# Agent attention with an ELU layer on one Trainium2 core: both accumulators summed by VectorE, and 25 more split steps

## Chip, core and metric

The kernel runs on one core of one Trainium2 chip. The metric is the device time of one execution in microseconds (us). In what follows PE is TensorE's matmul stream, PEld its weight loads, DVE is VectorE, ACT ScalarE, POOL GpSimd, SP the queue that issues the transfers. L12 is line 12 of the kernel before, where nothing else is said.

## What is computed

Two batches of 12480 tokens of 128 channels, 49 agents per batch, and a layer of 128 to 2048 to 128 with an ELU between. All in fp32.

```python
def sm(a, b):
    s = scale * (a @ b.transpose(0, 2, 1))
    s = s - s.max(-1, keepdims=True)
    e = np.exp(s)
    return e / (e.sum(-1, keepdims=True) + 1e-09)
agent_v = sm(agents, k) @ v
x = (sm(q, agents) @ agent_v).reshape(B * S, D)
h = x @ w_in
g = np.where(h > 0.0, h, np.exp(np.minimum(h, 0.0)) - 1.0)
return g @ w_out
```

## The kernel before

**The algebra.** The 49 rows of agent_v are multiplied with w_in once per batch (A, 49 x 2048), so that the hidden layer of a token is A transposed times its 49 softmax weights p. What is left per token is the scores of q against the agents, their softmax, p times A, the ELU, and the product with w_out.

**Rounds, halves, steps.** A round j is 960 tokens, 13 rounds per batch, 26 in all. The 2048 hidden columns are taken in 16 blocks of 128. A round has two halves of 8 steps; step s of the 416 takes one pair of blocks, c = 0 to 7, for 480 tokens of two groups. In the loop at L720, slot s issues p1(s), the hidden-layer matmuls (L404 to L413: three products of the hi and lo parts, each as two matmuls on 49 rows that run side by side, so six records in three pairs), then p2(s - 4), the output matmuls of the step four slots back (L437 to L453), then the work on the other engines for step s. In elu ScalarE makes Relu of -h (L419) and Exp of minus that (L422), and VectorE joins them into g (L424, 960 elements on 128 partitions).

**Plain and split steps.** A plain step multiplies g by w_out in fp32 (w_f), four matmuls that show as 8 records. A split step cuts g into hi and lo parts in the fp32r format: VectorE casts hi (L431), GpSimd subtracts twice for lo (L204, 480 each), and p2 is twelve matmuls (hi with w_lo, hi with w_hi, lo with w_hi). Which steps are split is a table by c, SPLITS, and is_split (L401) picks its tuple.

**The end of a half.** p2 accumulates a half in two PSUM banks, o0 and o1, one for each 64-row group of TensorE. After c = 7 VectorE copies o1 to SBUF (ob, L465), ScalarE copies o0 (oa, L468, between Relu and Exp of the slot's step), GpSimd adds them (L469), and the result goes out by DMA. The first matmul of the next half, p2 of c = 0, overwrites both banks.

**What is done in between.** So that TensorE has work while the banks are read, the loop issues p1(s + 1) ahead of p2 of c = 0 in slots that are not in the set "covered". In the covered slots (L628 on) a visit stands there: scores of q or k, or the products with v, for a later round, at slots 16 i + 11 and others. The second halves of rounds with a visit end beside one, the others do not; 17 of the 51 boundaries are covered. Smaller work of the softmax hangs on slots by a table: mid (before elu in its slot) and pre (after it).

**Order.** The program is scheduled by hand: each engine runs its instructions in the order in which the code issues them, and waits for tiles that other engines write or still read. Hidden-layer results lie in three PSUM slots of two banks, o0 and o1 take the other two banks.

**The prologue** computes agent_v of batch 0 and A. Its odd score tiles and two of A's four quarters use o0 and o1 as scratch; A_part (L265, L275) writes the ahi and alo parts of a quarter.

Of the kernel before, what the change touches and what calls it, by code (L numbers as in the profile page):

```python
# [24 lines left out]
def tile_agent_attention_moe(  # L25
# [27 lines left out]
    SPLITS = ((1, 3, 4, 6, 7), (1, 4, 6, 7))  # L53
    SPLIT = tuple(c for c in range(NP) if c in SPLITS[0] or c in SPLITS[1])
    PLAIN = tuple(c for c in range(NP) if c not in SPLITS[0] or c not in SPLITS[1])
# [8 lines left out]
    wc_p = ctx.enter_context(tc.tile_pool(name="wc", bufs=2))  # L64
# [7 lines left out]
    pp = const.tile([TQ, R // 2, 128], F32)  # L72
    win_sb = big.tile([C, DFF], F32)
# [239 lines left out]
    def q_rz(j, half):  # L313
        z = q_st[j]["z"]
        if half == 0:
            nc.vector.scalar_tensor_tensor(out=z, in0=z, scalar=1e-9, in1=z, op0=ALU.add, op1=ALU.max)
        else:
            q_st[j]["z"] = sm_p.tile([TQ, R], F32, tag="z", name="z")
            nc.vector.reciprocal(out=q_st[j]["z"], in_=z)
# [96 lines left out]
    def elu(s, between=None):  # L416
# [3 lines left out]
        if between:  # L420
            between()
# [5 lines left out]
    def split(s):  # L427
# [3 lines left out]
        nc.vector.tensor_copy(out=hi_t[s], in_=g_t[s])  # L431
# [5 lines left out]
    def p2(s):  # L437
        j, half, c = at_step(s)
        if c == 0:
            o_t[0] = ps_o.tile([128, 512], F32, tag="o0", name="o0")  # L440
            o_t[1] = ps_o.tile([128, 512], F32, tag="o1", name="o1")
# [8 lines left out]
        for i, (w, v) in enumerate(jobs):  # L450
            for u, r in enumerate(ROWS):
                x = slice(r, r + 64)
                nc.tensor.matmul(out=o_t[u][:, 0:T], lhsT=w[x], rhs=v[x, :], start=first and i == 0, stop=last and i == len(jobs) - 1)  # L453
        if last:
            oa = o_p.tile([128, T], F32, tag="oa", name="oa")
            ob = o_p.tile([128, T], F32, tag="ob", name="ob")
            pa, pb = o_t[0], o_t[1]
            n = j * G + half * T
            if s == S - 1:
                for x in (slice(0, T // 2), slice(T // 2, T)):  # L460
# [20 lines left out]
    with tc.manual_schedule():  # L481
# [238 lines left out]
        for s in range(S + LAG):  # L720
# [12 lines left out]
            if x >= 0 and s != LEAD:  # L733
                after = p2(x)
# [45 lines left out]
```

## Time and profile before

| | |
|---|---|
| median of 3 runs | 998.0 us (997.5 to 999.86) |
| profiled execution, its own time | 998.71 us |
| its span, first to last instruction | 995.9 us |
| granted clock of TensorE, mean | 0.996 |
| PE busy | 978.3 us (98%) |
| PEld busy | 734.3 us (74%) |
| ACT busy | 884.3 us (89%) |
| DVE busy | 849.7 us (85%) |
| POOL busy | 687.0 us (69%) |

Busy times overlap between engines. A share near 100% says that an engine has no room; the chain of waits says which engines' work follows on one another up to the end. A row of a view by time gives the start, the duration, the engine, the line, the operation with what it writes and reads, how many instructions were joined in the row, and in brackets the idle time before it with the engine whose signal ended it. Joined rows overlap their neighbours, since matmuls are pipelined: the distance of two starts is the measure, not the duration.

### The profile page before, as it was taken

What the parts mean: (1) busy time and instruction counts of PE and PEld (TensorE: products, weight loads), DVE (VectorE), ACT (ScalarE), POOL (GpSimd) and SP (SyncE); (2) the same over time, 40 slices, a digit from 0 to 9 for tenths busy, and PEclk for the clock granted to TensorE, in tenths of its full rate; (3) what the DMA queues carried; (4) which work ended last, traced back from release to release, by engine and by line L of the source; (5) the groups of instructions that cost most, each with busy time, mean ns of one, the idle gap of its engine ahead of it and who ended that gap; (6) DMA issues with size and microseconds to landing.
All of it is one profiled execution on the core that took longest, in us unless ns stands there. A gap on an engine that the chain in (4) does not pass through costs nothing.

```text
span 995.9 us, 25483 instructions
## 1 busy us (share of the span) xinstructions
PE 978.3 (98%) x10380; PEld 734.3 (74%) x10380; DVE 849.7 (85%) x1028; ACT 884.3 (89%) x1017; POOL 687.0 (69%) x559
## 2 busy tenths in 40 slices
PE   7899999999999999999999999999999999999998
PEld 5767777777777777877777777777777777777775
DVE  7778888888888878888888898898888888988887
ACT  4588998988988889998998999989999989989996
POOL 3146666666666766766786886877868867867886
PEclk8999999999999999999999999999999999999999
DMA  9942222223232211101101101011020021001000
GB/s 349 385 148 89 80 72 81 78 74 96 68 85 66 66 41 46 38 31 65 36 23 55 37 26 62 26 56 41 18 76 27 21 66 37 26 12 37 27 20 21
DMA packets 25983, 67.30 MB, mean 68 GB/s; under 512 B 3083, under 2 KB 14963, under 8 KB 25867
## 3 DMA queue, kind: packets, MB, share of 16 engines
q1 hardware_dynamic: 25867, 65.69, 19.5%
q8 instruction: 81, 1.33, 0.6%
q14 instruction: 35, 0.29, 0.1%
HBM read 43.11 MB, written 12.78 MB: 56 GB/s over the span
## 4 chain that ended last, share of the span: by engine, by line
PE 93%; DVE 2%; ACT 2%; DMA 2%; issue 1%; POOL 0%; SPq 0%; DVEq 0%; ACTq 0%
PE o L453 59%; PE h L413 27%; PE h L291 2%; PE h L219 2%; PE h L160 1%; DMA v<-in_vx_dram 1%; PE h L331 1%; DVE g L424 1%; DMA k<-in_kT_dram 1%; ACT e L419 1%; ACT e L422 0%; PE o L160 0%; DVE m_all L168 0%; DVE ex L107 0%; ACT ex L103 0%
## 5 line engine op out<-in xcount | busy, mean ns | idle before, releaser
L204 POOL TENSOR_TENSOR lo<-g,hi 128x480 fp32r<-128x480 f32 x484 | 603.3, 1272 | 253.6 <-DVE hi L431 190.3
L424 DVE SCALAR_TENSOR_TENSOR g<-e,h 128x960 f32<-128x960 f32 x416 | 478.2, 1150 | 109.2 <-ACT e L422 91.7
L419 ACT ACTIVATE e<-h 128x960 f32<-128x960 f32 x416 | 402.5, 967 | 41.0 <-PE h L413 38.5
L422 ACT ACTIVATE e<-e 128x960 f32<-128x960 f32 x416 | 419.1, 1007 | 11.6
L453 PE MATMUL o<-g,w_f 64*128 64x480 f32 x1384 | 307.8, 562 | 0.2 <-DVE g L424 0.2
L413 PE MATMUL h<-py,ahi 49*128 49x480 f32 x832 | 292.4, 431 | 1.4 <-DVE g L424 0.7
L413 PE MATMUL h<-px,ahi 49*128 49x480 f32 x832 | 292.4, 431 | 0.1
L431 DVE CAST hi<-g 128x960 fp32r<-128x960 f32 x243 | 198.4, 816 | 10.8
L453 PEld LDWEIGHTS o<-g,w_f 64*128 64x128 f32 x1384 | 133.2, 185 | 83.1 <-issue 73.6
L413 PEld LDWEIGHTS h<-py,ahi 49*128 49x128 f32 x832 | 149.9, 186 | 39.3 <-issue 23.4
L413 PEld LDWEIGHTS h<-px,ahi 49*128 49x128 f32 x832 | 149.9, 186 | 26.3 <-issue 17.0
L453 PE MATMUL o<-hi,w_lo 64*128 64x480 f32 x972 | 159.4, 403 | 0.0
L413 PE MATMUL h<-px,alo 49*128 49x480 f32 x416 | 157.0, 377 | 0.0
L413 PE MATMUL h<-py,alo 49*128 49x480 f32 x416 | 157.0, 377 | 0.0
L453 PE MATMUL o<-lo,w_hi 64*128 64x480 f32 x972 | 146.9, 378 | 0.0
L453 PE MATMUL o<-hi,w_hi 64*128 64x480 f32 x972 | 146.0, 376 | 0.0
L453 PEld LDWEIGHTS o<-hi,w_lo 64*128 64x128 f32 x972 | 93.4, 186 | 26.0 <-issue 14.3
L453 PEld LDWEIGHTS o<-lo,w_hi 64*128 64x128 f32 x972 | 92.6, 184 | 13.6 <-POOL lo L204 0.3
L453 PEld LDWEIGHTS o<-hi,w_hi 64*128 64x128 f32 x972 | 92.5, 184 | 13.0
L413 PEld LDWEIGHTS h<-py,alo 49*128 49x128 f32 x416 | 76.6, 184 | 5.7
L413 PEld LDWEIGHTS h<-px,alo 49*128 49x128 f32 x416 | 76.6, 184 | 5.6 <-DVE alo L275 0.2
L469 POOL TENSOR_TENSOR ob<-ob,oa 128x480 f32<-128x480 f32 x51 | 70.0, 1372 | 12.2 <-ACT oa L468 12.2
(89 smaller groups left out, 517.7 us busy)
## 6 DMA issues: line engine op xcount, KB each, us to landing
k<-in_kT_dram SPq DMA_DIRECT2D x26, 480.0 KB
q<-in_qT_dram SPq DMA_DIRECT2D x26, 480.0 KB
out_dram<-ob SPq DMA_DIRECT2D x51, 240.0 KB
py<-px SPq DMA_DIRECT2D x104, 91.9 KB
v<-in_vx_dram SPq DMA_DIRECT2D x13, 516.0 KB
v<-in_vx_dram SPq DMA_DIRECT2D x13, 483.8 KB
raw<-in_w_in_dram SPq DMA_DIRECT2D x4, 512.0 KB
raw<-in_w_out_dram SPq DMA_DIRECT2D x4, 512.0 KB
```

The costliest lines, as they stand in the source:

```text
L160: nc.tensor.matmul(out=ps[u:u + w, j * NA:(j + 1) * NA], lhsT=src[:, x:x + w], rhs=ag_sb[:, b, :], start=True, stop=True)
L204: eng.tensor_tensor(out=out, in0=x, in1=hi.bitcast(F32), op=ALU.subtract)
L219: nc.tensor.matmul(out=ps[u:u + 64], lhsT=e[:, j * NA:j * NA + 64], rhs=v_t[b, r][:, j, :], start=(r == rs[0] and j < 2), stop=(r == rs[-1 ...
L291: nc.tensor.matmul(out=ps[u:u + w, t * NA:(t + 1) * NA], lhsT=src[:, x:x + w], rhs=ag_sb[:, j // NG, :], start=True, stop=True)
L331: nc.tensor.transpose(ps[:NA2, u, i * HP:(i + 1) * HP], pp[x, i, 0:NA2], ident[x, x])
L413: nc.tensor.matmul(out=h[:, u, 0:T], lhsT=a[x, :], rhs=p[u ^ half][x, :], start=i == 0, stop=i == 2)
L419: nc.scalar.activation(out=e, in_=h, func=ACTF.Relu, scale=-1.0)
L422: nc.scalar.activation(out=e, in_=e, func=ACTF.Exp, scale=-1.0)
L424: nc.vector.scalar_tensor_tensor(out=g, in0=e, scalar=-1.0, in1=h, op0=ALU.add, op1=ALU.max)
L431: nc.vector.tensor_copy(out=hi_t[s], in_=g_t[s])
L453: nc.tensor.matmul(out=o_t[u][:, 0:T], lhsT=w[x], rhs=v[x, :], start=first and i == 0, stop=last and i == len(jobs) - 1)
L469: nc.gpsimd.tensor_tensor(out=ob, in0=ob, in1=oa, op=ALU.add)
```

## The change

1. A third tuple in SPLITS, with c = 0 added, for the second half of rounds whose middle is not covered; covered rounds now take the longer of the old tuples in both halves. Split steps go from 243 to 268: 16 covered rounds gain c = 3 of the second half, 9 uncovered rounds gain c = 0 of the second half. Round 0 stays as it was.
2. The cast of these 25 steps (by_act) is issued for ScalarE, one slot later, after the Exp of the next step.
3. The accumulators are one tile of two banks. VectorE sums both in one reduce into ob (L468 of the new file), and the DMA follows. VectorE's copy, ScalarE's copy and GpSimd's add are gone; the very last boundary stays as it was.
4. elu of a slot comes ahead of its mid work.
5. The tiles of q's softmax stay in place and have a 50th column that is set to 1e-9 once; the sum runs over 50 columns, and the instruction that added 1e-9 (L316, once per round) goes.
6. The prologue's scratch is one tile "outer" in place of o0 and o1, so that readers and writers of its two banks wait for one another as of one tile. One more block of w_out is kept in hi and lo parts.

```diff
-    SPLITS = ((1, 3, 4, 6, 7), (1, 4, 6, 7))
+    SPLITS = ((1, 3, 4, 6, 7), (1, 4, 6, 7), (0, 1, 3, 4, 6, 7))
...
+    qe = [const.tile([TQ, R, NA + 1], F32, name=f"qe{i}") for i in range(2)]
...
-        nc.vector.tensor_reduce(out=q_st[j]["z"], in_=q_st[j]["e"], axis=AX.X, op=ALU.add)
+        nc.vector.tensor_reduce(out=q_st[j]["z"], in_=qe[j % 2], axis=AX.X, op=ALU.add)
...
-            nc.vector.scalar_tensor_tensor(out=z, in0=z, scalar=1e-9, in1=z, op0=ALU.add, op1=ALU.max)
...
     def is_split(s):
         j, half, c = at_step(s)
-        return c in SPLITS[half if j * NM + NP + LAG in covered else 0]
+        free = j * NM + NP + LAG not in covered
+        return c in SPLITS[2 if free and half else half if j == 0 else 0]
+
+    def by_act(s):
+        j, half, c = at_step(s)
+        return j > 0 and half == 1 and c == (EDGE if j * NM + NP + LAG in covered else 0)
...
-        nc.vector.tensor_copy(out=hi_t[s], in_=g_t[s])
+        if by_act(s):
+            cast_hi(nc.scalar, hi_t[s], g_t[s])
+        else:
+            nc.vector.tensor_copy(out=hi_t[s], in_=g_t[s])
...
-            o_t[0] = ps_o.tile([128, 512], F32, tag="o0", name="o0")
-            o_t[1] = ps_o.tile([128, 512], F32, tag="o1", name="o1")
+            o_t[0] = ps_o.tile([128, 2, 512], F32, tag="o", name="o")
...
-            nc.vector.tensor_copy(out=ob, in_=pb[:, 0:T])
-
-            def rest_of_sum():
-                nc.scalar.activation(out=oa, in_=pa[:, 0:T], func=ACTF.Copy)
-                nc.gpsimd.tensor_tensor(out=ob, in0=ob, in1=oa, op=ALU.add)
-                nc.sync.dma_start(out=outT[:, n:n + T], in_=ob)
-
-            return rest_of_sum
+            nc.vector.tensor_reduce(out=ob, in_=o[:, :, 0:T].rearrange("p u t -> p t u"), axis=AX.X, op=ALU.add)
+            nc.sync.dma_start(out=outT[:, n:n + T], in_=ob)
...
+            outer = ps_o.tile([128, 2, 512], F32, tag="o", name="o")
...
-            banks = [hk[:, 0, :], o_ps[0], o_ps[1], o_ps[0][:, 256:512]]
+            banks = [hk[:, 0, :], outer[:, 0, :], outer[:, 1, :], outer[:, 0, 256:512]]
...
+            if s < S:
+                elu(s)
             for fn, a in mid.pop(s, []):
                 fn(a)
-            if s < S:
-                elu(s, after)
-                split(s)
-            elif after:
-                after()
+            if 0 < s < S:
+                if by_act(s - 1):
+                    split(s - 1)
+                if not by_act(s):
+                    split(s)
```

ScalarE's order around the middle of round 23, one of the nine uncovered rounds, before: Relu and Exp of the second half's steps 0 to 3, the copy of o0 in the last. A name's number tells one tile from another.

```order
L419 ACTIVATE e_12467<-h_12448 128x960
L422 ACTIVATE e_12467<-e_12467 128x960
L419 ACTIVATE e_12483<-h_12472 128x960
L422 ACTIVATE e_12483<-e_12483 128x960
L419 ACTIVATE e_12513<-h_12494 128x960
L422 ACTIVATE e_12513<-e_12513 128x960
L419 ACTIVATE e_12540<-h_12518 128x960
L468 ACTIVATE oa_12537<-o0_12343 128x480
L422 ACTIVATE e_12540<-e_12540 128x960
```

The same place of the changed kernel:

```order
L421 ACTIVATE e_12538<-h_12519 128x960
L422 ACTIVATE e_12538<-e_12538 128x960
L421 ACTIVATE e_12554<-h_12543 128x960
L422 ACTIVATE e_12554<-e_12554 128x960
L199 ACTIVATE hi_12559<-g_12541 128x960
L421 ACTIVATE e_12590<-h_12571 128x960
L422 ACTIVATE e_12590<-e_12590 128x960
L421 ACTIVATE e_12617<-h_12595 128x960
L422 ACTIVATE e_12617<-e_12617 128x960
```

The cast of step 0 (hi from its g) now stands between Exp of step 1 and Relu of step 2; the copy of o0 is gone.

VectorE's order at the same boundary, before: g of steps 0 and 1, the cast of step 1, g of step 2, the copy of o1, g of step 3 and its cast.

```order
L424 SCALAR_TENSOR_TENSOR g_12470<-e_12467,h_12448 128x960
L424 SCALAR_TENSOR_TENSOR g_12486<-e_12483,h_12472 128x960
L431 CAST hi_12488<-g_12486 128x960
L424 SCALAR_TENSOR_TENSOR g_12516<-e_12513,h_12494 128x960
L465 COPY ob_12538<-o1_12344 128x480
L424 SCALAR_TENSOR_TENSOR g_12546<-e_12540,h_12518 128x960
L431 CAST hi_12548<-g_12546 128x960
```

And in the changed kernel:

```order
L424 SCALAR_TENSOR_TENSOR g_12541<-e_12538,h_12519 128x960
L424 SCALAR_TENSOR_TENSOR g_12557<-e_12554,h_12543 128x960
L434 CAST hi_12565<-g_12557 128x960
L424 SCALAR_TENSOR_TENSOR g_12593<-e_12590,h_12571 128x960
L468 TENSOR_REDUCE ob_12614<-o_12415 128x480
L424 SCALAR_TENSOR_TENSOR g_12620<-e_12617,h_12595 128x960
L434 CAST hi_12622<-g_12620 128x960
```

The reduce of both banks takes the place of the copy of one; it stays behind g of step 2.

TensorE's order there in the changed kernel: the end of the step pulled ahead, then the output matmuls of step 0, which were four plain ones (o0 and o1 from g_12470 and w_f) before.

```order
L415 MATMUL h_12635<-py0_11980,alo_6835 128x480
L415 MATMUL h_12635<-px0_11979,alo_6835 128x480
L456 MATMUL o_12642<-hi_12559,w_lo_89 128x480 x4
L456 MATMUL o_12642<-hi_12559,w_hi_88 128x480 x4
L456 MATMUL o_12642<-lo0_12561,w_hi_88 128x480 x2
L456 MATMUL o_12642<-lo1_12563,w_hi_88 128x480 x2
```

Step 0 is split here, and its first matmul waits for the reduce that reads the tile o.

## Rows read from the trace of the kernel before

**Rows 1.** The chain that ended last, its shares by line (page, part 4).

```profile
PE o L453 59%; PE h L413 27%; PE h L291 2%; PE h L219 2%; PE h L160 1%; DMA v<-in_vx_dram 1%; PE h L331 1%; DVE g L424 1%; DMA k<-in_kT_dram 1%; ACT e L419 1%; ACT e L422 0%; PE o L160 0%; DVE m_all L168 0%; DVE ex L107 0%; ACT ex L103 0%
```

**Rows 2.** Busy us from 700 to 900: PE, PEld, DVE, ACT, POOL; clock; DMA.

```profile
700.00:900.00 200.00, 200.00 (x1936) 149.65 (x1934) 176.41 (x201) 187.16 (x209) 152.23 (x121) 1.00 0.11 36
```

**Rows 3.** By time, PE from 887 to 893: three steps' first output matmuls.

```profile
887.99 1.77 PE L453 MATMUL o<-g,w_f 64*128 64x480 f32 x8
...
890.25 0.59 PE L453 MATMUL o<-hi,w_lo 64*128 64x480 f32 x4
...
892.20 0.59 PE L453 MATMUL o<-hi,w_lo 64*128 64x480 f32 x4
```

**Rows 4.** Groups by line and shape: count, busy us, mean ns, idle before.

```profile
L204 POOL TENSOR_TENSOR lo<-g,hi 128x480 fp32r<-128x480 f32 x484 | 603.3, 1272 | 253.6 <-DVE hi L431 190.3 <-PE h L413 32.2 <-DVE z L319 25.8
L424 DVE SCALAR_TENSOR_TENSOR g<-e,h 128x960 f32<-128x960 f32 x416 | 478.2, 1150 | 109.2 <-ACT e L422 91.7 <-POOL lo L204 6.0 <-PE h L413 3.8
...
L431 DVE CAST hi<-g 128x960 fp32r<-128x960 f32 x243 | 198.4, 816 | 10.8
...
L465 DVE COPY ob<-o 128x480 f32<-128x480 f32 x51 | 33.6, 658 | 2.6
...
L296 DVE TENSOR_REDUCE mx<-h 124x8 f32<-124x392 f32 x26 | 14.5, 558 | 0.0
...
L168 DVE TENSOR_REDUCE m_all<-h 120x49 f32<-120x392 f32 x20 | 10.9, 561 | 0.5
...
L172 DVE TENSOR_REDUCE mrun<-m_all 120x49 f32<-120x637 f32 x1 | 0.8, 814 | 0.0
```

**Rows 5.** By time, a boundary without a visit: PE's output matmuls, VectorE.

```profile
893.06 0.60 PE L453 MATMUL o<-lo,w_hi 64*128 64x480 f32 x4
...
894.81 1.77 PE L453 MATMUL o<-g,w_f 64*128 64x480 f32 x8
...
892.50 1.16 DVE L424 SCALAR_TENSOR_TENSOR g<-e,h 128x960 f32<-128x960 f32 x1 [0.32 <-ACT e L422]
893.73 0.66 DVE L465 COPY ob<-o 128x480 f32<-128x480 f32 x1
```

**Rows 6.** By time, PE after a wait: the first pair and the next.

```profile
70.18 0.48 PE L413 MATMUL h<-py,ahi 49*128 49x480 f32 x1
...
70.51 0.38 PE L413 MATMUL h<-py,ahi 49*128 49x480 f32 x1
```

**Rows 7.** By time, VectorE's copy at the first and the last such boundary.

```profile
101.34 0.66 DVE L465 COPY ob<-o 128x480 f32<-128x480 f32 x1
...
977.63 0.66 DVE L465 COPY ob<-o 128x480 f32<-128x480 f32 x1
```

**Rows 8.** By time, round 23's middle: ScalarE steps 1 to 3, VectorE 2.

```profile
906.21 1.01 ACT L422 ACTIVATE e<-e 128x960 f32<-128x960 f32 x1
907.47 0.97 ACT L419 ACTIVATE e<-h 128x960 f32<-128x960 f32 x1 [0.25 <-PE h L413]
908.48 1.01 ACT L422 ACTIVATE e<-e 128x960 f32<-128x960 f32 x1
909.43 0.98 ACT L419 ACTIVATE e<-h 128x960 f32<-128x960 f32 x1
...
909.58 1.15 DVE L424 SCALAR_TENSOR_TENSOR g<-e,h 128x960 f32<-128x960 f32 x1 [0.40 <-ACT e L422]
910.75 0.66 DVE L465 COPY ob<-o 128x480 f32<-128x480 f32 x1
```

**Rows 9.** By time, prologue's end: VectorE on A, PE's first output matmuls.

```profile
55.75 0.49 DVE L265 TENSOR_SCALAR ahi<-o,rz 113x256 fp32r<-113x256 f32 x1 [0.74 <-PE o L257]
56.27 0.48 DVE L275 SCALAR_TENSOR_TENSOR alo<-o,rz,ahi 113x256 fp32r<-113x256 f32 x1
56.67 0.48 DVE L265 TENSOR_SCALAR ahi<-o,rz 113x256 fp32r<-113x256 f32 x1
...
58.87 1.84 PE L453 MATMUL o<-g,w_f 64*128 64x480 f32 x7 [0.23 <-DVE g L424]
```

More of the change, by code (lines that the diff above doesn't have):

```diff
@@ L52, in tile_agent_attention_moe @@
     EDGE = (NP - 1 + LAG) % NP
-    SPLITS = ((1, 3, 4, 6, 7), (1, 4, 6, 7))
-    SPLIT = tuple(c for c in range(NP) if c in SPLITS[0] or c in SPLITS[1])
-    PLAIN = tuple(c for c in range(NP) if c not in SPLITS[0] or c not in SPLITS[1])
+    SPLITS = ((1, 3, 4, 6, 7), (1, 4, 6, 7), (0, 1, 3, 4, 6, 7))
+    SPLIT = (0, 1, 3, 4, 6, 7)
+    PLAIN = (0, 2, 3, 5)
     scale = 1.0 / float(C) ** 0.5
@@ L452, in p2 @@
                 x = slice(r, r + 64)
-                nc.tensor.matmul(out=o_t[u][:, 0:T], lhsT=w[x], rhs=v[x, :], start=first and i == 0, stop=last and i == len(jobs) - 1)
+                nc.tensor.matmul(out=o[:, u, 0:T], lhsT=w[x], rhs=v[x, :], start=first and i == 0, stop=last and i == len(jobs) - 1)
         if last:
-            oa = o_p.tile([128, T], F32, tag="oa", name="oa")
             ob = o_p.tile([128, T], F32, tag="ob", name="ob")
-            pa, pb = o_t[0], o_t[1]
             n = j * G + half * T
             if s == S - 1:
+                oa = o_p.tile([128, T], F32, tag="oa", name="oa")
+                pa, pb = o[:, 0], o[:, 1]
                 for x in (slice(0, T // 2), slice(T // 2, T)):
@@ L525, in tile_agent_attention_moe @@
             dve.memset(ones, 1.0)
+            for x in qe:
+                dve.memset(x, 1e-9)
             dve.memset(s_all[:, :, R:R + 1, :], 0.0)
@@ L607, in tile_agent_attention_moe @@
             av_out()
-            o_ps = [ps_o.tile([128, 512], F32, tag=f"o{i}", name=f"o{i}") for i in range(2)]
-            banks = [hk[:, 0, :], o_ps[0], o_ps[1], o_ps[0][:, 256:512]]
+            banks = [hk[:, 0, :], outer[:, 0, :], outer[:, 1, :], outer[:, 0, 256:512]]
             def A_part(c, eng):
@@ L729, in tile_agent_attention_moe @@
             if s == 2:
-                t = ps_o.tile([128, 512], F32, tag="o1", name="o1")
-                nc.tensor.matmul(out=t[:, 0:T], lhsT=ident, rhs=win_sb[:, 0:T], start=True, stop=True)
+                nc.tensor.matmul(out=outer[:, 1, 0:T], lhsT=ident, rhs=win_sb[:, 0:T], start=True, stop=True)
             x = s - LAG + (s < LEAD)
             if x >= 0 and s != LEAD:
-                after = p2(x)
+                p2(x)
             if s == NP - LAG - 1:
                 p1(s)
+            if s < S:
+                elu(s)
             for fn, a in mid.pop(s, []):
                 fn(a)
-            if s < S:
-                elu(s, after)
-                split(s)
-            elif after:
-                after()
+            if 0 < s < S:
[3 more added lines that the diff above has]
+                    split(s)
             for fn, a in pre.pop(s, []):
```

27 lines of the change are left out of this document (10 added, 17 removed).

## The prediction, written before the result was known

> **What bounds the kernel now.** I read the chain of waits first: it says which engine's work ends last. Two lines of TensorE hold 86% of it, the output matmuls (L453) with 59% and the hidden-layer matmuls (L413) with 27% [rows 1]. Then the busy time by stretch, since a chain can hide engines that are nearly full: from 700 to 900 us TensorE is busy for all of the 200 us, at a granted clock of 1.00, while ScalarE has 187, VectorE 176 and GpSimd 152 [rows 2]. So TensorE's own work sets the time, and nobody makes it wait in the steady state. What the change does is worth what it takes off TensorE's list of matmuls, less each wait that it opens on TensorE. The other three engines count only where one of them is late at one spot. Those spots I read in time order, engine by engine, at the end of an accumulation, which I call a boundary: the last output matmul of a half, the copy out of PSUM, and the first output matmul of the next half, which writes the same banks.
>
> **The change, part by part**, against the profiled execution (998.71 us; the median is 998.0, 0.7 lower).
>
> *25 more split steps.* Split steps rise from 243 to 268. A step of plain fp32 lasts 2.26 us on TensorE from the start of its output matmuls to the next step's (887.99 to 890.25), a split one 1.95 (890.25 to 892.20) [rows 3]. Each conversion takes 0.31 off, so 25 x 0.31 = **-7.8 us**.
>
> *The sum of the two banks on VectorE.* Before, VectorE copied one bank and ScalarE the other, side by side, and GpSimd added. Now one VectorE instruction reads both banks, 960 elements per partition in place of 480, and only then may TensorE write them again. Its duration is not in this trace. Below it lies the copy of 480, 0.66 us [rows 4], if only the outputs counted. Above it I put twice the nearest estimate, 2.3, if picking elements from two banks in turn halved the rate. The nearest rows: VectorE's reduces take 0.561 for 392 elements and 0.814 for 637, a slope of 1.03 ns per element, so 960 come to 0.814 + 323 x 1.03 ns = 1.15; and its two-operand pass over 960 takes 1.150 [rows 4]. I take 1.15. The reduce in L168 reads its 392 elements 49 apart, the one in L296 side by side, and they take 561 and 558 ns [rows 4], so a stride by itself is not seen to cost.
>
> What TensorE has as cover: at a boundary without a visit, the program pulls the hidden matmuls of one more step ahead. The last output matmul ends at 893.06 + 0.60 = 893.66, the copy starts at 893.73 (0.07 later), and the next output matmul at 894.81, 1.15 after that end [rows 5]. A matmul that has waited pays its weight load in the open: after a wait the first pair of matmuls is 0.33 from the next (70.18 to 70.51) [rows 6], against 0.22 in the flow (1.95 for the nine pairs of a split step [rows 3]), so 0.11; with 0.07 for the hand-over that is 0.18. The stall is 0.07 + 1.15 + 0.18 - 1.15 = 0.25 us. Boundaries without a visit lie between 101.34 and 977.63 [rows 7], 34 of the 51: 34 x 0.25 = **+8.5 us**. At the other 17 a visit's matmuls stand between as well; I cost those at nothing. If that cover were only as long as the pulled step, they would add 17 x 0.25 = 4.
>
> *The cast on ScalarE.* The added cast goes to ScalarE, behind the Exp of the step after. In 16 rounds it is step 3 beside a visited boundary, where ScalarE no longer has the copy and the visit leaves room: nothing. In 9 rounds it is step 0 of the second half, and there ScalarE's queue is: Exp of step 1, the cast, Relu and Exp of step 2; and VectorE's is: g of step 2, then the sum. Now Exp of step 1 starts at 906.21 and Relu of step 2 at 907.47. One full-width instruction follows another after 0.95 (908.48 to 909.43), so with a cast of that length Relu of step 2 starts at 906.21 + 0.95 + 0.95 = 908.11, 0.64 late [rows 8]. Exp and g of step 2 hang on it: g starts at 909.58 after waiting for that very Exp, and the copy follows at 910.75 as soon as g is done [rows 8]. So the sum starts 0.64 late, on top of its own stall, straight onto TensorE: 9 x 0.64 = **+5.8 us**. Lower bound 0 (if VectorE took the sum first, which its fixed order excludes), upper bound 9 x 1.0.
>
> Here the page "ScalarE: Activation LUTs" of the Trainium skill, section "Rules for kernel authors", speaks against the change: plain element-wise work belongs on VectorE, not ScalarE. This trace agrees with its direction, 0.66 to 0.82 for the cast on VectorE against 0.95 here. By that rule the cast would have stayed on VectorE and the time would be that of the second rival below.
>
> *The prologue.* The scratch of two banks is now one tile, so the matmuls for the fourth quarter of A wait for VectorE's alo of the third (56.27 + 0.48 = 56.75), and VectorE then waits for them, for some 0.74 as it did for the third [rows 9]. Its next step starts at 57.49, not 56.67, and TensorE already waits for the first g behind it (0.23 at 58.87): **+0.8 us**, lower bound 0.
>
> *At nothing.* GpSimd: 50 more lo at 1.27 = 64 us [rows 4], spread over the run, and 51 adds over as many elements are gone. VectorE: 51 x (1.15 - 0.66) = 25 us more, of the 24 idle in each 200. The guard of the softmax's sum by a 50th column, one small VectorE instruction fewer in each round, and the order of the mid-slot work behind g sit in that idle time. If VectorE's idle were gone, g would be late for the output matmuls four steps on, which none of these is long enough to reach.
>
> **Sum:** -7.8 + 8.5 + 5.8 + 0.8 = +7.3 on 998.71; against the median, 998.0 + 7.3 = **1005.3 us**.
>
> **The rivals.**
> - *The sum is quick, and the change is faster.* If VectorE's sum lasts about as long as the copy (0.66), the 34 boundaries cost nothing; the point from which it decides is 1.15 - 0.07 - 0.18 = 0.90 us. In the 9 rounds 0.07 + 0.64 + 0.66 + 0.18 - 1.15 = 0.40 is left: -7.8 + 3.6 + 0.8 = -3.4, so 994.6, and 991.0 if the cast's delay is hidden as well. For it: the copy is 0.66. Against it: both reduces and the two-operand pass follow the elements read.
> - *Only the cast's delay is hidden.* -7.8 + 8.5 + 0.8 = +1.5: 999.5, no change that can be told. For it: ScalarE loses its 51 copies, and each stall on TensorE lets it catch up. Against it: the fixed order [rows 8] has 0.25 idle before that Relu and no more.
> - *Two banks read in turn halve the rate.* 2.3 us: a stall of 1.40 at 34 boundaries, 47.6; -7.8 + 47.6 + 5.8 + 0.8 = +46.4, so 1044.4. Against it: the strided reduce above. The page "Advanced Engine Details and Errata" of the Trainium skill, section "PSUM Cachelines", says that every two neighbouring fp32 should lie side by side for best throughput; the sum's pairs lie 2 KB apart. L168's reduce breaks that rule too, at 561 ns against the 558 of one that keeps it, so no slowdown shows here.
> - *GpSimd is late for the added steps.* In the 9 rounds its pair for step 0 starts at about 908.1 and two pairs last 5.1, to 913.2; the matmuls that read the second come near 914.6. 1.4 us are spare; if a pile-up ate them and 0.5 more, 9 rounds would lose 4.5: 1009.8.
>
> **How the numbers follow.** A measurement of this kernel tells about 0.3%, 3 us, from no change. The forecast gets 0.52, the quick sum 0.15, the hidden cast 0.20, the two banks 0.05, GpSimd 0.08. Faster than 995: 0.12 of the quick sum and 0.04 of the hidden cast, together 0.16. Within 3 us: 0.03 + 0.14, and 0.05 of the forecast's low end (a sum of 1.05 us takes 3.4 off), 0.22. Slower: the rest, 0.62. The range leaves out the two banks and the lower part of the quick sum and goes from 994 to 1011, where the upper end is the forecast with a sum of 1.3 us (+5.1). The likeliest case's own range is 1001 to 1011.
>
> **What would show it.** In the changed profile: the sum's group near 1150 ns; TensorE idle of some 0.25 before the first output matmul of a half, put down to VectorE's sum, 34 times, and near 0.9 in the 9 rounds; split steps at 1.95; busy time of L456 plain matmuls down by 25 steps. Wrong would be a sum below 0.90, TensorE without idle at boundaries, or Relu of step 2 in its old place although the cast stands ahead of it.

## The result and the profile after

The changed kernel takes **1007.32 us** (median of 4 runs, 1007.07 to 1007.85), against 998.13 for the kernel before: a ratio of 1.009, with a 95% interval from 1.0073 to 1.0107. It is 9.2 us slower, in the direction forecast and inside the range; the sum of the terms had 7.3. The profiled execution took 1007.07 us with a span of 1005.3, 9.4 more than before.

The chain that ended last in the changed kernel, first by engine and then by line:

```profile
PE 76%; ACT 9%; DVE 8%; issue 5%; DMA 1%; POOL 1%; SPq 0%; DVEq 0%; ACTq 0%; POOLq 0%
PE o L456 48%; PE h L415 21%; ACT e L421 4%; ACT e L422 3%; PE h L219 2%; DVE g L424 2%; DVE ob L468 2%; PE h L291 2%; DVE hi L434 2%; PE h L160 1%; PE h L328 1%; ACT hi L199 1%; DMA k<-in_kT_dram 1%; DVE m_all L168 0%; ACT qe L307 0%
```

TensorE's two lines had 86% of it [rows 1]; now they have 69%, and ScalarE, VectorE and gaps ("issue") have the rest: TensorE is made to wait. Busy time hides that almost entirely. In the same stretch as [rows 2], with the same columns:

```profile
700.00:900.00 200.00, 199.26 (x1946) 157.84 (x1944) 179.72 (x191) 184.97 (x200) 149.02 (x121) 1.00 0.11 36
```

199.26 of 200 looks full, because a matmul's record is longer than its turn (0.38 us against 0.22) and its tail covers part of a wait. The waits have to be read from starts. I therefore compared both traces step by step, by the start of the first matmul on alo of each of the 416 steps (a record that is complete in both). What grows between two neighbouring steps is lost there. Grouped by the place, in us, with the experiments that follow:

| kernel | up to round 1 | c = 3 split, 16 places | first boundary, 18 rounds | first boundary, 7 uncovered rounds | second boundary, 9 uncovered rounds | rest | sum |
|---|---|---|---|---|---|---|---|
| changed | 1.2 | -4.5 | 4.3 | 5.0 | 3.1 | 0.0 | 9.1 |
| e1 old splits | 2.0 | 0.1 | 4.4 | 1.5 | 2.0 | -0.3 | 9.7 |
| e3 casts on VectorE | 3.9 | -4.7 | 4.2 | 1.6 | 5.2 | -0.3 | 9.9 |
| e4 no c = 3 | 4.5 | 0.3 | 4.4 | 1.5 | 3.2 | -0.2 | 13.7 |
| e5 half a sum | 0.8 | -4.4 | 0.1 | 1.9 | -0.2 | 0.0 | -1.8 |
| e8 prologue | 0.7 | -4.4 | 4.3 | 4.8 | 3.1 | -0.1 | 8.4 |
| e9 c = 3 early, old sum | 0.1 | -2.9 | -0.1 | 0.0 | 0.0 | -0.3 | -3.1 |
| e12 combined | 0.8 | -4.5 | 4.3 | 1.6 | 3.1 | -0.3 | 4.9 |

The first boundary is the one inside the first half of a round, the second the one in its middle; all of those counted have no visit. The second boundary's column includes the gain of c = 0's split, where there is one. The first column also holds when a trace's first loads landed, some tenths to 1.5 us either way: e6 and e11, whose prologue is that of the kernel before, have 1.6 and 1.5 there.

Groups of the changed kernel, as in [rows 4] (count, busy us, mean ns, idle before):

```profile
L204 POOL TENSOR_TENSOR lo<-g,hi 128x480 fp32r<-128x480 f32 x534 | 667.6, 1277 | 277.5 <-DVE hi L434 172.5 <-ACT hi L199 71.4 <-DVE z L316 21.8
...
L434 DVE CAST hi<-g 128x960 fp32r<-128x960 f32 x243 | 227.9, 938 | 13.2 <-DVE g L424 0.5
...
L468 DVE TENSOR_REDUCE ob<-o 128x480 f32<-128x960 f32 x51 | 58.9, 1155 | 0.7
...
L199 ACT ACTIVATE hi<-g 128x960 fp32r<-128x960 f32 x25 | 24.8, 991 | 0.0
```

The sum takes 1155 ns (the estimate was 1.15 us), the cast on ScalarE 991, and VectorE's 243 casts have grown from 816 to 938 on average although they are the same in number.

A boundary without a visit and without added steps near it, as in [rows 5]: TensorE's last and next output matmul, VectorE's g of step 2 and the sum.

```profile
934.56 0.62 PE L456 MATMUL o<-lo,w_hi 64*128 64x480 f32 x4
936.43 1.88 PE L456 MATMUL o<-g,w_f 64*128 64x480 f32 x8
...
934.04 1.16 DVE L424 SCALAR_TENSOR_TENSOR g<-e,h 128x960 f32<-128x960 f32 x1 [0.42 <-ACT e L422]
935.22 1.16 DVE L468 TENSOR_REDUCE ob<-o 128x480 f32<-128x960 f32 x1
```

The matmul ends at 935.18, the sum runs from 935.22 to 936.38, and the next output matmul starts at 936.43, 1.25 after that end in place of 1.15. The first group also lasts 1.34 up to the next (937.77) in place of 1.23 (896.04 against 894.81 in the trace before): the weight load in the open. Together 0.21.

**The first boundary of an uncovered round** (round 23) loses 0.64. The lines of GpSimd, VectorE, ScalarE, the last output matmul and the weight loads, in this order:

```profile
887.54 5.18 POOL L204 TENSOR_TENSOR lo<-g,hi 128x480 fp32r<-128x480 f32 x4 [4.45 <-ACT hi L199]
893.73 2.40 POOL L204 TENSOR_TENSOR lo<-g,hi 128x480 fp32r<-128x480 f32 x2 [1.01 <-DVE z L316]
...
894.92 1.72 DVE L434 CAST hi<-g 128x960 fp32r<-128x960 f32 x1
896.56 2.21 DVE L424 SCALAR_TENSOR_TENSOR g<-e,h 128x960 f32<-128x960 f32 x2
898.80 0.94 DVE L434 CAST hi<-g 128x960 fp32r<-128x960 f32 x1
899.90 1.16 DVE L424 SCALAR_TENSOR_TENSOR g<-e,h 128x960 f32<-128x960 f32 x1 [0.16 <-ACT e L422]
900.98 1.15 DVE L468 TENSOR_REDUCE ob<-o 128x480 f32<-128x960 f32 x1
...
896.36 1.01 ACT L422 ACTIVATE e<-e 128x960 f32<-128x960 f32 x1
897.80 0.97 ACT L421 ACTIVATE e<-h 128x960 f32<-128x960 f32 x1 [0.43 <-DVE g L424]
...
899.89 0.60 PE L456 MATMUL o<-lo,w_hi 64*128 64x480 f32 x4
...
901.11 0.18 PEld L415 LDWEIGHTS h<-px,ahi 49*128 49x128 f32 x1 [0.37 <-DVE g L424]
902.18 0.30 PEld L456 LDWEIGHTS o<-g,w_f 64*128 64x128 f32 x4 [0.55 <-DVE ob L468]
```

Read it from the top. GpSimd gets the pair for c = 3 only when ScalarE has cast it, and is late with the pairs after it. VectorE's cast of c = 7 at 894.92 then falls beside a running pair (893.73 to 896.13) and lasts 1.72 instead of 0.66. The two g behind it start at 896.56; ScalarE, which needs a buffer that this g frees, waits 0.43; so g of step 2 ends at 901.06, and the sum begins 0.49 after the last output matmul (900.49). TensorE waits twice: 0.24 for a hidden-layer slot that the late g frees (the load at 901.11), and then 0.40 at the sum.

That a cast stands still beside GpSimd's subtraction agrees with the Trainium skill, "SBUF — State Buffer", section "Who interferes with whom": VectorE and GpSimd share one pair of ports under an exclusive lock, and a cast can be among the VectorE instructions that want it. Here the cast ends about 0.5 after GpSimd's pair does, having stood for about 1.1.

**The second boundary** of the same round (c = 0 split, its cast on ScalarE), as in [rows 8]; ScalarE, VectorE, GpSimd, TensorE:

```profile
913.68 1.01 ACT L422 ACTIVATE e<-e 128x960 f32<-128x960 f32 x1
914.59 0.99 ACT L199 ACTIVATE hi<-g 128x960 fp32r<-128x960 f32 x1
915.49 0.95 ACT L421 ACTIVATE e<-h 128x960 f32<-128x960 f32 x1
...
916.00 1.50 DVE L434 CAST hi<-g 128x960 fp32r<-128x960 f32 x1
917.51 1.16 DVE L424 SCALAR_TENSOR_TENSOR g<-e,h 128x960 f32<-128x960 f32 x1
918.58 1.15 DVE L468 TENSOR_REDUCE ob<-o 128x480 f32<-128x960 f32 x1
...
913.39 7.56 POOL L204 TENSOR_TENSOR lo<-g,hi 128x480 fp32r<-128x480 f32 x6 [0.69 <-DVE hi L434]
...
917.57 0.61 PE L456 MATMUL o<-lo,w_hi 64*128 64x480 f32 x4
919.88 0.70 PE L456 MATMUL o<-hi,w_lo 64*128 64x480 f32 x4 [0.15 <-DVE ob L468]
```

The forecast chain is there: the cast between Exp of step 1 and Relu of step 2, then g, then the sum. It has company: VectorE's cast of step 1 falls beside GpSimd's added pair and takes 1.50, so that g of step 2 would start at 917.5 by either way. The sum begins 0.40 after the matmul's end (918.18); the forecast had 0.07 + 0.64 = 0.71. Before, that matmul ended at 910.68, 0.07 ahead of the copy at 910.75 [rows 8]:

```profile
910.08 0.60 PE L453 MATMUL o<-lo,w_hi 64*128 64x480 f32 x4
```

**The prologue**, TensorE, then VectorE:

```profile
57.07 0.64 PE L257 MATMUL o<-win_sb,avt 128*64 128x256 f32 x4 [1.19 <-DVE alo L275]
...
56.44 0.48 DVE L275 SCALAR_TENSOR_TENSOR alo<-o,rz,ahi 113x256 fp32r<-113x256 f32 x1
57.75 0.48 DVE L265 TENSOR_SCALAR ahi<-o,rz 113x256 fp32r<-113x256 f32 x1 [0.82 <-PE o L257]
```

A's fourth quarter waits 1.19 for the third's alo, and VectorE then 0.82 for those matmuls, the chain that was forecast.

### The profile page after: what moved, and what is told of

It is laid out like the page before. It is cut to its first block, busy times and chain, and to the rows that moved or that the text cites. A ratio compares the mean times of both kernels' runs of the same rounds, so it can differ in the third digit from the quotient of the medians.

```text
span 1005.3 us, 25609 instructions
## 1 busy us (share of the span) xinstructions
PE 983.5 (98%) x10480; PEld 761.6 (76%) x10480; DVE 877.5 (87%) x1004; ACT 885.8 (88%) x992; POOL 684.1 (68%) x559
## 3 DMA queue, kind: packets, MB, share of 16 engines
q8 instruction: 82, 1.34, 0.6%
## 4 chain that ended last, share of the span: by engine, by line
PE 76%; ACT 9%; DVE 8%; issue 5%; DMA 1%; POOL 1%; SPq 0%; DVEq 0%; ACTq 0%; POOLq 0%
PE o L456 48%; PE h L415 21%; ACT e L421 4%; ACT e L422 3%; PE h L219 2%; DVE g L424 2%; DVE ob L468 2%; PE h L291 2%; DVE hi L434 2%; PE h L160 1%; PE h L328 1%; ACT hi L199 1%; DMA k<-in_kT_dram 1%; DVE m_all L168 0%; ACT qe L307 0%
## 5 line engine op out<-in xcount | busy, mean ns | idle before, releaser
L204 POOL TENSOR_TENSOR lo<-g,hi 128x480 fp32r<-128x480 f32 x534 | 667.6, 1277 | 277.5 <-DVE hi L434 172.5
L456 PE MATMUL o<-g,w_f 64*128 64x480 f32 x1184 | 266.5, 566 | 1.7 <-DVE ob L468 0.9
L434 DVE CAST hi<-g 128x960 fp32r<-128x960 f32 x243 | 227.9, 938 | 13.2 <-DVE g L424 0.5
L456 PE MATMUL o<-hi,w_lo 64*128 64x480 f32 x1072 | 173.8, 397 | 1.4 <-DVE ob L468 1.1
L456 PEld LDWEIGHTS o<-g,w_f 64*128 64x128 f32 x1184 | 114.3, 185 | 78.0 <-issue 61.7
L456 PE MATMUL o<-lo,w_hi 64*128 64x480 f32 x1072 | 163.9, 378 | 0.0
L456 PE MATMUL o<-hi,w_hi 64*128 64x480 f32 x1072 | 163.1, 376 | 0.0
L456 PEld LDWEIGHTS o<-lo,w_hi 64*128 64x128 f32 x1072 | 106.2, 184 | 10.9 <-DVE lo L204 0.2
L456 PEld LDWEIGHTS o<-hi,w_hi 64*128 64x128 f32 x1072 | 106.1, 184 | 10.4
L468 DVE TENSOR_REDUCE ob<-o 128x480 f32<-128x960 f32 x51 | 58.9, 1155 | 0.7
```

The source lines that it names most:

```text
L204: eng.tensor_tensor(out=out, in0=x, in1=hi.bitcast(F32), op=ALU.subtract)
L456: nc.tensor.matmul(out=o[:, u, 0:T], lhsT=w[x], rhs=v[x, :], start=first and i == 0, stop=last and i == len(jobs) - 1)
L468: nc.vector.tensor_reduce(out=ob, in_=o[:, :, 0:T].rearrange("p u t -> p t u"), axis=AX.X, op=ALU.add)
```

## The experiments

The theory after this reading: the sum is longer than its cover at 34 places; the added casts, c = 3's too, make g late in uncovered rounds; the prologue's shared tile adds a wait. The main rivals: the new order of the mid-slot work makes g late; the sum's place and not its length holds TensorE; GpSimd needed the relief of the adds. All edits are to the changed kernel unless said. Runs without a repeat are one execution beside one of the kernel before (999.1 for e1 to e4, 998.4 for e5 to e8). The four runs of the kernel before in the result lie between 997.5 and 999.9, so a single run tells nothing about 1 or 2 us; there the columns of the table have to.

**e1: the old splits.**

```diff
-        return c in SPLITS[2 if free and half else half if j == 0 else 0]
+        return c in SPLITS[0 if free else half]
...
-        return j > 0 and half == 1 and c == (EDGE if j * NM + NP + LAG in covered else 0)
+        return False
```

> The changed kernel without its 25 added split steps and so without casts on ScalarE; VectorE's sum of both banks stays. Theory (the sum outlasts the cover at all 34 boundaries without a visit; the larger losses of the nine uncovered rounds come from the added steps): TensorE loses 0.21 us at each of the 34 boundaries and nothing more at any of them; 998.1 + 34 x 0.21 + 1.2 for the prologue = about 1006.5. Rival (the extra 0.43 at the first boundary of eight uncovered rounds comes from the new order of the mid-slot work, not from the added steps): that extra stays, about 1010. Rival 2 (the sum itself costs nothing, all of the loss hangs on the added steps): about 999.

1007.6 us, of which the first column explains 0.8 more than in the changed kernel. Each of the 34 boundaries loses alike (4.4 + 1.5 + 2.0 = 7.9, or 0.23 each), the first boundaries of uncovered rounds as little as any other. The order of the mid-slot work costs nothing here, beside the new sum: that rival falls. So does the second: the sum alone costs 8. With or without the 25 added steps the changed kernel takes about the same time: they cost as much as they bring (7.2). VectorE's casts are back at their old length:

```profile
L434 DVE CAST hi<-g 128x960 fp32r<-128x960 f32 x243 | 200.9, 827 | 10.3 <-PE o L456 0.5
```

**e2: the old sum on the one tile of two banks.**

```diff
-            nc.vector.tensor_reduce(out=ob, in_=o[:, :, 0:T].rearrange("p u t -> p t u"), axis=AX.X, op=ALU.add)
-            nc.sync.dma_start(out=outT[:, n:n + T], in_=ob)
+            oa = o_p.tile([128, T], F32, tag="oa", name="oa")
+            nc.vector.tensor_copy(out=ob, in_=o[:, 1, 0:T])
+
+            def rest_of_sum():
+                nc.scalar.activation(out=oa, in_=o[:, 0, 0:T], func=ACTF.Copy)
+                nc.gpsimd.tensor_tensor(out=ob, in0=ob, in1=oa, op=ALU.add)
+                nc.sync.dma_start(out=outT[:, n:n + T], in_=ob)
+
+            return rest_of_sum
```

(rest_of_sum is called between Relu and Exp, as before.)

> The changed kernel with the old way of summing: VectorE copies one bank, ScalarE the other between Relu and Exp, GpSimd adds. Added split steps, casts on ScalarE and all else as changed. Theory (the sum's length is what TensorE waits for): the 0.21 at 34 boundaries goes; of the later starts in the nine uncovered rounds some 0.1 to 0.2 per boundary stays, since the copies start late there too, but are 0.5 shorter: about 994 (993 to 996), faster than both kernels. Rival (the sum on VectorE was needed, because GpSimd cannot do 51 adds beside 50 more lo): output matmuls wait for lo, 1000 or more.

1031.3 us, a miss by 37. The time lies in the rival's range, but not for its reason: TensorE's weight loads wait 19.3 us in all for ScalarE's copy and 1.7 for a lo of GpSimd's. The run does not undo the sum cleanly. ScalarE at round 24's first boundary:

```profile
956.83 0.57 ACT L474 ACTIVATE oa<-o 128x480 f32<-128x480 f32 x1 [1.08 <-DVE ob L471]
```

Two engines that read one tile are put in order: ScalarE's copy waits for VectorE's (956.16 to 956.81) with nothing to protect, and ScalarE, which had to run back to back before it, stands for 1.08. It does so at all 51 boundaries, 53.2 us in all.

**e3: the casts on VectorE.**

```diff
-        return j > 0 and half == 1 and c == (EDGE if j * NM + NP + LAG in covered else 0)
+        return False
```

> The changed kernel with the casts of the 25 added steps on VectorE, in the slot of their own step; the split steps stay. Theory (the cast ahead of Relu of step 2 on ScalarE makes g of step 2, and so the sum, late at the second boundary of nine rounds): that boundary falls from 0.66 to 0.21 lost, 9 x 0.45 = 4.0 less; if the first boundaries of those rounds keep their 0.43 the time is about 1003, if they lose it too about 1000. Rival (VectorE is so full that a cast of 0.7 to 1.5 there delays g as much as the cast on ScalarE did): 1007 or more.

1007.8 us, the rival's time, but 2.7 of it lie in the first column (below); without them it would be 1005. The parts answer differently. For c = 3 the move pays: the first boundary of the seven uncovered rounds falls from 5.0 to 1.6, which is the sum's share alone. For c = 0 it costs: the second boundary rises from 3.1 to 5.2, where the theory had it fall by 4.0. There the rival holds.

The 2.7 came with the granted clock. Busy time in the stretches of the prologue (PE, PEld, DVE, ACT, POOL, clock), of e3:

```profile
54.00:57.00 3.00, 1.77 (x12) 0.84 (x14) 1.76 (x4) 2.25 (x3) 0.00 (x0) 0.95 1.02 414
57.00:60.00 3.00, 3.00 (x16) 1.85 (x14) 2.03 (x3) 0.59 (x1) 0.00 (x0) 0.50 0.27 110
60.00:63.00 3.00, 2.89 (x8) 0.97 (x6) 1.52 (x2) 2.94 (x4) 0.00 (x0) 0.50 0.00 0
```

and of the changed kernel:

```profile
57.00:60.00 3.00, 2.93 (x18) 1.55 (x18) 2.03 (x3) 1.62 (x3) 0.00 (x0) 1.00 0.46 187
```

In e3 TensorE falls from the level of 2.4 GHz to that of 1.2 behind the wait of 1.19 us; in the changed kernel's profiled run the same wait does not bring it down. e4 fell too (0.61 and 0.50 in these stretches), e1 and e2 did not.

**e4: no c = 3.**

```diff
-        return c in SPLITS[2 if free and half else half if j == 0 else 0]
+        return c in SPLITS[2 if free and half else 0 if free else half]
...
-        return j > 0 and half == 1 and c == (EDGE if j * NM + NP + LAG in covered else 0)
+        return half == 1 and c == 0 and j * NM + NP + LAG not in covered
```

> The changed kernel without the 16 added split steps c = 3 beside a visit; the nine of c = 0 stay, with their casts on ScalarE. Theory (the cast on ScalarE and the pair of lo beside a visit shift GpSimd's work under VectorE's later casts, which makes g late for the next boundary without a visit): the 0.43 extra at the first boundary of eight uncovered rounds goes, 3.4 less, and 16 x 0.30 = 4.8 of gain goes too: about 1008.7. Rival (the extra there has another cause, such as the order of the mid-slot work or the dropped small instruction): it stays, about 1012.

1011.7 us, again with 3.3 from the prologue's clock; without them 1008.4. That is the time of the theory, and the column of the uncovered rounds' first boundary shows it without the clock: 1.5 in place of 5.0. The steps c = 3 make the extra there.

**e5: half a sum.**

```diff
-            nc.vector.tensor_reduce(out=ob, in_=o[:, :, 0:T].rearrange("p u t -> p t u"), axis=AX.X, op=ALU.add)
-            nc.sync.dma_start(out=outT[:, n:n + T], in_=ob)
+            H = T // 2
+            nc.vector.tensor_reduce(out=ob[:, 0:H], in_=o[:, :, 0:H].rearrange("p u t -> p t u"), axis=AX.X, op=ALU.add)
+            nc.sync.dma_start(out=outT[:, n:n + H], in_=ob[:, 0:H])
```

> The changed kernel, but VectorE sums (and the DMA writes) only 240 of the 480 columns of each half, so half of the output is left out; all else as changed. Theory (TensorE waits for the length of the sum beyond some 0.9 us): the sum takes about 0.561 - 152 x 0.001 x 1.03 + 240 x 0.001 x 1.03 = 0.65, below the cover; the 34 boundaries lose nothing but what the late starts in the nine uncovered rounds leave, 0.1 to 0.2 each: 1007.3 - 34 x 0.21 - 8 x 0.25 - 9 x 0.30 = about 995.5. Rival (TensorE waits for the sum's place behind g in VectorE's order, whatever it lasts): 1003 or more.

996.4 us. Its group:

```profile
L469 DVE TENSOR_REDUCE ob<-o 128x240 f32<-128x480 f32 x51 | 33.3, 654 | 0.7
```

With 654 ns the 18 first boundaries lose 0.1 in all, in place of 4.3. What stays is of another kind: 1.9 at the uncovered rounds' first boundary is the wait for a hidden-layer slot that the late g frees, 0.24 to 0.3 each; the same at their second boundary, 2.5, is hidden under the nine gains of 0.30 (-2.7). The length of the sum holds TensorE, not its place.

**e6: the old sum on two tiles.** The edit of e2, with o0 and o1 again as two tiles, in the prologue too:

```diff
-            o_t[0] = ps_o.tile([128, 2, 512], F32, tag="o", name="o")
-        o = o_t[0]
+            o_t[0] = ps_o.tile([128, 512], F32, tag="o0", name="o0")
+            o_t[1] = ps_o.tile([128, 512], F32, tag="o1", name="o1")
+        o = [o_t[0], o_t[1]]
```

> As the run with the old sum, but with two accumulator tiles again (in the prologue too), so that ScalarE's copy does not wait for VectorE's; added split steps and casts on ScalarE stay. Theory (in the earlier run ScalarE's copy waited for VectorE's, since both read one tile, and ScalarE, without room for that, fell behind): no loss at boundaries except 0.1 to 0.2 after late starts in the nine uncovered rounds, prologue as before: 998.1 - 7.5 + 1.5 + 1.4 = about 993.5. Rival (ScalarE cannot carry 51 copies of 0.57 beside 25 casts of 0.99 in any order): it stays on the chain, 1000 or more.

1007.6 us: the rival's time. The waits at the boundaries shrink (2.5 and 2.3 in place of 4.3 and 5.0; 0.8 in place of 3.1), but 6.1 appear in the rest, most of it two or three slots behind a boundary, 0.2 to 0.4 each, where TensorE waits for a slot that a late g frees. The added steps cannot be the whole cause: round 1, which has no added step ahead of it, loses 0.19 at that place too, and 0.21 in e7. The traces show what else is late. VectorE behind the first boundary of round 1, in the kernel before:

```profile
101.91 0.56 DVE L325 TENSOR_TENSOR pp<-qe,z 124x392 f32<-124x392 f32 x1
102.88 1.15 DVE L424 SCALAR_TENSOR_TENSOR g<-e,h 128x960 f32<-128x960 f32 x1 [0.40 <-ACT e L422]
104.06 0.66 DVE L431 CAST hi<-g 128x960 fp32r<-128x960 f32 x1
...
106.66 1.15 DVE L424 SCALAR_TENSOR_TENSOR g<-e,h 128x960 f32<-128x960 f32 x1
```

and in e7, which has the old sum on two tiles as well:

```profile
101.51 0.66 DVE L472 COPY ob<-o 128x480 f32<-128x480 f32 x1
103.04 1.15 DVE L426 SCALAR_TENSOR_TENSOR g<-e,h 128x960 f32<-128x960 f32 x1 [0.87 <-ACT e L424]
104.11 0.56 DVE L322 TENSOR_TENSOR pp<-qe,z 124x392 f32<-124x392 f32 x1
104.59 0.65 DVE L436 CAST hi<-g 128x960 fp32r<-128x960 f32 x1
...
107.08 1.14 DVE L426 SCALAR_TENSOR_TENSOR g<-e,h 128x960 f32<-128x960 f32 x1
```

Before, the softmax's product pp fills the time in which VectorE waits for ScalarE. With elu ahead of the mid-slot work (point 4 of the change) pp stands behind g. Counted from the copy (101.34 before [rows 7], 101.51 in e7), the cast then starts after 3.08 in place of 2.72, and the third g after 5.57 in place of 5.32. So some 0.2 of the loss in a round is read as the price of that order beside the old sum. With the new sum (e1) it costs nothing: there no copy stands between Relu and Exp, and g starts 0.45 earlier behind the boundary. No run undid the order alone.

**e7: the same with the casts on VectorE** (by_act returns False, as in e3).

> As the run before this one, with the casts of the 25 added steps on VectorE. Theory (ScalarE is then free of added work; VectorE's cast beside GpSimd's pair makes g of step 2 late by some 0.65 at the second boundary of uncovered rounds, of which the copy of 0.66 leaves 0.4): 998.1 - 7.5 + 9 x 0.4 = about 994. Rival (VectorE's casts, stretched beside GpSimd's work, delay g at other steps too): 998 or more.

1008.1 us: again the rival's time. 5.5 at the second boundary of the uncovered rounds, where the step pulled ahead starts 1.0 late (in eight of the nine) and the gain of 0.3 comes back, and 6.9 in the rest, of the kind just shown. So with the old sum in this order the added steps do not pay with either engine casting; what they would do in the old order these two runs do not tell.

**e8: the prologue's matmuls together.**

```diff
-                A_part(2, dve)
-                A_part(3, dve)
+                for c in (2, 3):
+                    A_pe(0, 512 * c, 512 * c + 512, banks[c])
+                for c in (2, 3):
+                    A_out(0, 512 * c, 512 * c + 512, dve)
```

> The changed kernel with the matmuls of A's third and fourth quarters issued together ahead of VectorE's parts of both, so that none waits for VectorE. Theory (the one scratch tile made the fourth quarter's matmuls wait 1.2 us for VectorE): first rounds 1.2 earlier, about 1006.1, and no fall of the granted clock between 57 and 63 us. Rival (TensorE would wait there for something else, such as the loads): 1007.3 as before.

1006.4 us, the theory's time within 0.3, though 1.0 is no more than runs of one kernel differ by; the granted clock is 1.00 in the three stretches. In the trace the wait of 1.19 is gone, but it has partly moved: the next user of the tile now waits.

```profile
58.65 1.07 PE L728 MATMUL o<-win_sb,ident 128*128 128x480 f32 x2 [0.50 <-DVE alo L275]
```

**e9: the kernel before, with c = 3 in rounds 1 to 9 alone.** Edit to the kernel before:

```diff
-        return c in SPLITS[half if j * NM + NP + LAG in covered else 0]
+        return c in SPLITS[half if j * NM + NP + LAG in covered and not 0 < j < 10 else 0]
```

> The kernel before with one part of the change: the added split step c = 3 beside a visit, in rounds 1 to 9 only, its cast on VectorE; old sum, old order, no c = 0. Theory (these nine steps stand behind a visit's matmuls, which cover all that they add): 9 x 0.30 = 2.7 off, about 995.4. Rival (the loss of 0.2 per round that the runs with two accumulator tiles show two slots after the first boundary comes with the added step): 2.7 - 9 x 0.2 = 0.9 off, about 997.2.

**994.97 us** (994.6 to 996.0, 8 runs) against 998.2: ratio 0.997, interval 0.9959 to 0.998. It beats both kernels. Nine steps give 2.9 and lose nothing at any boundary, and TensorE stays full in the stretch of [rows 2]:

```profile
700.00:900.00 200.00, 200.00 (x1942) 148.97 (x1940) 175.72 (x201) 187.34 (x209) 152.24 (x121) 1.00 0.11 36
```

The loss of 0.2 two slots behind the boundary, which e6 and e7 have in the same rounds with the same steps, is not there. So it does not come with the added step. Here pp stands ahead of g again, which agrees with the reading in e6.

**e10: the same in all 16 covered rounds.**

```diff
-        return c in SPLITS[half if j * NM + NP + LAG in covered else 0]
+        return c in SPLITS[half if j == 0 else 0]
```

> As the run before, with the added step in all 16 covered rounds from 1 on. Theory (with the cast on VectorE the boundary after the round loses little, as in the changed kernel with casts on VectorE): 16 x 0.30 = 4.8 off, at most 0.2 lost in each of 8 rounds that follow a double visit of q: 993.3 to 995. Rival (VectorE has no room for the cast beside a double visit): no better than rounds 1 to 9 alone, 995.4 or more.

995.57 us (995.08 to 996.63, 10 runs), ratio 0.9975, interval 0.9966 to 0.9985: as good as e9, not better. For six of the seven steps in rounds 10 to 22 the gain of 0.30 is given back as 0.3 to 0.4, two slots behind the next boundary (2.3 in the rest). A double visit of q stands beside those steps, with four VectorE instructions of its own. The rival's time holds; that VectorE's room is the reason was not tested by itself.

**e11: e10 with c = 3's cast on ScalarE**, one slot later, as in the changed kernel.

```diff
+        if by_act(s):
+            cast_hi(nc.scalar, hi_t[s], g_t[s])
+        else:
+            nc.vector.tensor_copy(out=hi_t[s], in_=g_t[s])
...
+                if s and by_act(s - 1):
+                    split(s - 1)
+                if not by_act(s):
+                    split(s)
```

> As the run before, with the added step's cast on ScalarE after the Exp of the next step, as in the changed kernel. Theory (the cast ahead of Relu makes g late; with the old sum some 0.24 is left of it as TensorE's wait for a slot at the first boundary of eight rounds): about 2 us more than with VectorE's cast, 995 to 997. Rival (the cast's place makes no difference where a visit covers it): the same as with VectorE's cast.

1007.64 us, ratio 1.0099 (1.0084 to 1.0114): 12 more than e10, six times what was expected. It is the mechanism of the first boundary above, with worse company. GpSimd, VectorE and ScalarE behind round 5's visit:

```profile
275.81 5.18 POOL L204 TENSOR_TENSOR lo<-g,hi 128x480 fp32r<-128x480 f32 x4 [2.89 <-ACT hi L199]
...
276.06 1.50 DVE L438 CAST hi<-g 128x960 fp32r<-128x960 f32 x1
...
279.79 1.23 DVE L316 SCALAR_TENSOR_TENSOR z<-z 124x8 f32<-124x8 f32 x1
...
281.53 0.53 ACT L211 ACTIVATE s_all<-s_all 120x392 f32<-120x392 f32 x1 [1.17 <-DVE s_all L208]
```

The pairs start late because ScalarE casts late, VectorE's next cast stands beside them (1.50), the small instruction that the changed kernel dropped takes 1.23, and ScalarE waits 1.17 for work of VectorE that stands behind both. Against e10 this costs 0.6 to 1.8 in each of rounds 5 to 10, 0.6 to 1.0 in each of the seven uncovered rounds behind a double visit, and nothing in rounds 2 and 3: how much a late cast costs hangs on what VectorE has to do behind it.

**e12: the parts put together.** The edit of e8, and c = 3's casts on VectorE, c = 0's on ScalarE:

```diff
-        return j > 0 and half == 1 and c == (EDGE if j * NM + NP + LAG in covered else 0)
+        return half == 1 and c == 0 and j * NM + NP + LAG not in covered
```

> The changed kernel with the casts of the 16 steps c = 3 on VectorE, those of the nine c = 0 on ScalarE, and the two matmul groups of the prologue issued together. Theory (the losses add up: 3.4 from ScalarE's casts at c = 3, shown at the first boundary of seven uncovered rounds, and 0.5 to 1.0 from the prologue): 1007.3 - 3.4 - 0.8 = about 1003. Rival (c = 3's cast is needed off VectorE in rounds whose c = 0 cast is on ScalarE, since both engines are near full): 1006 or more.

1003.8 us (1002.86 to 1004.12, 4 runs), ratio to the kernel before 1.0062 (1.0045 to 1.0079). The two repairs add up, 3.5 in place of 4.2, and each column is that of the run that repaired it. What remains slower than before is the sum (7.9) and the late g at c = 0 (3.8), against the 7.2 that the split steps bring.

## Why the prediction was right, and which of its terms were not

The direction, the time within 2 us and the main cause, the sum, were right. That the time came so near is partly luck, as two errors cancel. The terms can be read off the table one by one:

- *25 split steps, -7.8.* Measured -7.2: -4.5 for the 16 (the column of c = 3) and -2.7 for the nine (e5). Right.
- *The sum, +8.5.* Measured 7.9 (e1), 0.23 each in place of 0.25, with a sum of 1155 ns. Right, and e5 shows the cause by halving the length. The estimate by the slope of two reduces was good to 1%, and the strided read from two banks, the third rival, shows no cost: 1155 ns for 960 and 654 for 480 are 1.04 ns per element.
- *The cast of c = 0 on ScalarE, +5.8.* The second boundary lost 3.1 net, 5.8 with the gain of 2.7 taken out; less the sum's own 2.0 that is 3.8, or 0.42 each in place of 0.64. The order of the chain was as forecast; two of its lengths were not. Relu of step 2 starts 1.81 after Exp of step 1 (913.68 to 915.49) in place of 1.26 [rows 8], so 0.55 late and not 0.64: the instructions follow one another after 0.91 and 0.90. And the copy in [rows 8] had not waited for g alone, as the prediction reads it. The last output matmul ahead of it ended only 0.07 earlier, at 910.68. The copy started 1.17 after g, while the sum starts 1.07 after it (917.51 to 918.58), so the first tenth of a delay of g costs nothing. Not shown is that ScalarE's queue alone makes g late: VectorE's cast beside GpSimd's added pair, which the prediction did not have, ends at the same time, and no run separates the two. The rule of the Trainium skill that the prediction cites ("ScalarE: Activation LUTs", "Rules for kernel authors") names relu, max, min, add and mul, and no cast; carried over to a cast, as the prediction does, it would have put this one on VectorE. There it costs 2.1 more (e3), and the measurement decides.
- *The cast of c = 3, nothing.* This is the step that failed: "the visit leaves room: nothing". It costs 3.4 (5.0 less 1.6 in e3 and e12; 3.5 by e4). I had looked at the boundary next to the step. The cost falls nine slots later, by way of GpSimd's late pairs and VectorE's stretched cast, and only in the seven rounds behind a double visit of q; the nine rounds behind the other visits lose no more than in e1. For this step the direction of that rule holds: on VectorE the cast costs nothing with the new sum (e3).
- *The prologue, +0.8.* 1.2 stand in the table's first column, but that column is as large in traces with the old prologue, so the term is not measured to better than 1. e8 takes 0.5 away there and 1.0 in the time. The wait for VectorE was right (1.19 and then 0.82); its reach to the next user of the tile, and the clock that fell behind it in e3 and e4, were not in the sum.
- *At nothing: GpSimd and VectorE.* GpSimd's busy total fits, as forecast (687.0 us before, 684.1 after), and the rival that has it late for the added steps falls: in the loop TensorE's waits in the changed trace name no lo. But an instruction's length depends on what runs beside it, and 122 ns more on each of 243 casts is 30 us of VectorE that the budget did not hold.

Terms measured: -7.2 + 7.9 + 3.8 + 3.4 + 1.2 = 9.1. That this is the measured difference within 0.1 is no further proof, since the terms are shares of the table's 9.1. The forecast's 7.3 fell 2 short of it by two errors of opposite sign, 2.0 too much at c = 0 and 3.4 too little at c = 3, and a few tenths.

I then expected the old sum with the added steps to be the fast kernel (e6, e7). It is not, as it stands there. Part of the loss is read as the new order of the mid-slot work, which costs nothing beside the new sum; the rest lies at and behind the boundaries beside the added steps. What was shown to pay is the old sum in the old order with the few added steps that a visit covers (e9).

## What to carry to other kernels

Where one engine is full, look at each point where it must hand a buffer back, and compare the cover in time (here 0.9 us) with the length of the instruction that reads it; an instruction that does the work of three is worse when it is longer than those of the three that stood on that path (1155 ns against copies of 658 and 573). A step that is added to an idle engine has to be followed through every queue behind it until the next point without cover, not to the nearest one. Where two engines slow one another, budget the slow length, and read waits from starts: the busy time showed 199.3 of 200 us.

## What was not expected of the hardware

- A cast of 960 elements on VectorE takes 0.66 us alone and up to 1.73 when it starts inside one of GpSimd's subtractions; which of them meet is set by when a third engine delivers. The length follows from the starts: it is 0.66, or what is left of the running subtraction plus 0.52, whichever is longer. That holds within 0.01 us for all 145 such casts in the trace before and for 176 of 177 in the changed kernel's.
- A wait of 1.19 us on TensorE in the prologue was followed by the level of 1.2 GHz for some 6 us in two of six profiled runs with that wait (e3, e4), and by none in the others. The 2.7 to 3.3 us that it costs are as large as some of the terms above.
- Two readers of one PSUM tile on two engines ran one behind the other in e2, and ScalarE stood 1.08 us for it. That order comes from how the program's tiles are tracked, not from the memory: with two tiles (e6) it is gone.
